# Ten plain float32 heads instead of sixteen, weights decoded in three Vector pieces, and 13 slots without a head between the two kinds of heads

## The chip, the cores and the metric

One core of a Trainium2 chip runs the kernel. The metric is the device time of one execution in microseconds, the median of several runs. Engines are named as in the profile: PE is the tensor engine (PEld its weight loads), DVE is Vector, ACT is ScalarE, POOL is GpSimd, SP issues the DMAs. Each engine takes its instructions in the order in which the program gives them.

## The reference

Gated causal attention over 64 heads (8 batches of 8 heads, 576 tokens, 64 columns), then a normalised two-layer block on the 4608 tokens of 512 columns. The two weight matrices reach the kernel as 64-bit floats.

```python
def _attn_ref(q, k, v, f):
    scores = scale * np.matmul(q, k.transpose(0, 1, 3, 2))
    cum = np.cumsum(np.log(np.clip(f, 0.0001, 1.0)), axis=-1)
    scores = np.where(causal, -1e9, scores + cum[..., :, None] - cum[..., None, :])
    attn = np.exp(scores - np.max(scores, axis=-1, keepdims=True))
    return np.matmul(attn / (np.sum(attn, axis=-1, keepdims=True) + 1e-09), v)

def _moe_ref(x, g_ln, w_ch1, w_ch2):
    xn = (x - mu) / np.sqrt(var + 1e-06) * g_ln
    return x + np.maximum(xn @ w_ch1, 0.0) @ w_ch2
```

## The kernel before

**Slots.** The work is a list of slots, each a row tile t (1 to 4) of one head: 64 heads make slots 0 to 255, and three empty ones follow. In a slot the letters of a string in `ORDERS` say which pieces are given to the engines, and in which order:

- Q: score products (PE, L357 in a plain head, L359 and L360 in a split one); S: row minima (DVE, L373); e: exponentials (ACT, L384); B: row sums and normalised rows (DVE L389 and L390, POOL L391).
- t, h, l: transposes of the tile `LAG` = 2 slots before (PE, L397), their copy or first part (ACT, L447), their second part (DVE, L452, split heads alone).
- A, F, a: product with v (PE, L460 plain, L482 split), its columns, out to DRAM (L513, L516, L527, L529).
- M, r, m, N: a step of the second layer. M is the first product (12 matmuls, L566 to L568), r and m its two parts (ACT L574, DVE L579), N the second product of the step before (6 matmuls, L588 to L590). R takes the tokens' rows and loads and splits the next chunk's tokens (L543, L550, L551).
- W: a tick of the weights; f, g, w: some of its Vector pieces; s: column sums (PE, L191); P: operands of the next heads.

**Two kinds of heads.** A head with n < `NFULL` is plain: its products take float32 operands as they are. Any other is split: each operand is two float32r parts, made by ACT, DVE and POOL (L329, L330, L335 to L337, L343, L344), and there are more products of a cheaper kind. The parts of split heads lie in a pool that opens where the weights' pool closes, so the first heads are plain.

**Weights.** There are 32 items of 128 x 512 (16 for each layer). A tick decodes one from 64-bit words: ACT scales its high words (L160), then four Vector pieces (L176, L177, L180, L172), of which the last is followed by an addition on POOL (L173). An item of the first layer then has its column sums made on PE and four centring pieces on DVE (L199). ACT makes the first part (L215), POOL the second (L219). A tick starts when the slot's due count says so: `W_SLOTS` = 2.82 slots per tick until slot 37, 1.1 ticks per slot from there. Step j needs the items up to 2(j + 1).

**Steps.** From slot 35 on a slot holds one step if there is one. 18 chunks of 256 tokens have 16 steps each, 288 in all. A chunk can start when its tokens are written: chunks 0 and 1 after batch 0 (heads 0 to 7), 2 and 3 after batch 1 (heads 8 to 15). What is left after the last slot, 72 steps, runs alone.

## Time and profile before

| | |
|---|---|
| median of 3 runs | 1277.68 us (1275.74 to 1287.45) |
| span of the profiled execution | 1274.4 us (its time beside the span is not listed) |
| PE, DVE, ACT, POOL busy | 1248.6, 848.8, 639.4, 455.2 us |
| slot 4, 36, 58 and 256 start | at 20.0, 100.2, 216.1 and about 1049 us |
| DMA | 90.96 MB |

A slot's start is read as the start of its first score product in the order of time. The span runs from the first to the last instruction; the median of the runs lies 3.3 us above it.

### The profile page before, as it was taken

The page shows a single profiled execution, that of the slowest core. Times are in us where ns is not written, and L with a number is a line of the kernel's source. Part 1 is how long each engine was busy: PE and PEld are TensorE (multiplying, and loading weights), DVE is VectorE, ACT ScalarE, POOL GpSimd, SP SyncE. Part 2 cuts the span into 40 slices and gives each one's busy share as a digit, 9 for nine tenths or more (in the row PEclk, how much of TensorE's full clock was granted, in tenths as well). Part 3 has the DMA queues.
Part 4 walks back from the last instruction along what each step waited for, and adds up shares of the span by engine and source line. Part 5 has one row for each costly group of instructions (what it writes and reads, how often), then busy time and mean ns, then how long its engine had stood idle before and what let it go on. Part 6 is the DMA issues. An engine that isn't in the chain of part 4 may idle for free.

```text
span 1274.4 us, 24837 instructions
## 1 busy us (share of the span) xinstructions
PE 1248.6 (98%) x8292; PEld 1087.5 (85%) x8292; DVE 848.8 (67%) x2948; ACT 639.4 (50%) x1904; POOL 455.2 (36%) x543
## 2 busy tenths in 40 slices
PE   8999889999999999999999999999999999999998
PEld 5656667789899999999999989899999999999997
DVE  6889997367676767686868687777777773233232
ACT  5776455455555555555555565555555552112111
POOL 4666665234343333433333444333434330000000
PEclk8999998999999999999999999999999999999999
DMA  5444341122212222222222212222222200100100
GB/s 167 141 129 138 123 150 49 47 70 75 75 62 62 76 75 74 71 79 72 78 70 68 77 58 66 64 75 75 75 74 75 69 33 26 34 26 9 34 17 17
DMA packets 65904, 90.96 MB, mean 71 GB/s; under 512 B 15856, under 2 KB 50672, under 8 KB 65776
## 3 DMA queue, kind: packets, MB, share of 16 engines
q1 hardware_dynamic: 65776, 89.37, 22.4%
q8 instruction: 66, 1.08, 0.4%
q14 instruction: 62, 0.51, 0.1%
HBM read 70.17 MB, written 19.17 MB: 70 GB/s over the span
## 4 chain that ended last, share of the span: by engine, by line
PE 85%; DVE 9%; DMA 2%; issue 2%; ACT 1%; POOL 1%; SPq 0%; POOLq 0%; DVEq 0%; ACTq 0%
PE h L566 10%; PE h L567 10%; PE h L568 10%; PE acc L588 10%; PE acc L589 10%; PE acc L590 10%; PE tr L397 8%; PE o L482 5%; PE s L359 3%; PE s L360 3%; PE o L460 2%; DVE wy L177 2%; PE s L357 2%; DVE wr L180 1%; DVE wr L176 1%
## 5 line engine op out<-in xcount | busy, mean ns | idle before, releaser
L566 PE MATMUL h<-x,w1h 128*128 128x256 f32 x1152 | 329.0, 286 | 0.8 <-DVE st L389 0.7
L391 POOL TENSOR_SCALAR p<-p,st 64x64 f32<-64x64 f32 (+4 forms) x320 | 179.0, 564 | 417.4 <-DVE st L390 175.0
L567 PE MATMUL h<-x,w1h 128*128 128x256 f32 x1152 | 326.5, 283 | 1.5 <-DVE x L551 1.5
L568 PE MATMUL h<-x,w1l 128*128 128x256 f32 x1152 | 325.1, 282 | 0.0
L574 ACT ACTIVATE hh<-h 128x256 fp32r<-128x256 f32 x288 | 110.7, 384 | 292.4 <-PE h L568 291.9
L588 PE MATMUL acc<-w2h,hh 128*128 128x512 f32 x576 | 228.9, 397 | 0.0
L589 PE MATMUL acc<-w2l,hh 128*128 128x512 f32 x576 | 227.8, 396 | 0.0
L579 DVE SCALAR_TENSOR_TENSOR hh<-h,hh 128x256 fp32r<-128x256 f32 x288 | 121.0, 420 | 157.3 <-ACT hh L574 152.3
L590 PE MATMUL acc<-w2h,hh 128*128 128x512 f32 x576 | 225.0, 391 | 0.0
L567 PEld LDWEIGHTS h<-x,w1h 128*128 128x128 f32 x1152 | 219.5, 191 | 6.2 <-DVE x L551 1.7
L566 PEld LDWEIGHTS h<-x,w1h 128*128 128x128 f32 x1152 | 218.9, 190 | 6.1 <-DVE st L389 1.4
L568 PEld LDWEIGHTS h<-x,w1l 128*128 128x128 f32 x1152 | 219.2, 190 | 0.0
L384 ACT ACTIVATE p<-p,st 64x64 f32<-64x64 f32 (+4 forms) x320 | 178.9, 560 | 76.7 <-DVE st L373 75.1
L447 ACT CAST ph<-tr 64x128 fp32r<-64x128 f32 (+4 forms) x384 | 109.2, 334 | 135.5 <-PE tr L397 122.8
L397 PE MATMUL tr<-identr,p 128*128 128x128 f32 (+2 forms) x896 | 147.1, 274 | 10.1 <-POOL p L391 8.9
L397 PEld LDWEIGHTS tr<-identr,p 128*128 128x128 f32 (+2 forms) x896 | 97.0, 130 | 51.4 <-POOL p L391 17.8
L452 DVE TENSOR_TENSOR ph<-tr,ph 64x192 fp32r<-64x192 f32 x192 | 57.7, 301 | 117.5 <-ACT ph L447 114.2
L373 DVE CUSTOM_DVE_ANT_0 p<-s,mask 64x64 f32<-64x64 f32 (+4 forms) x320 | 130.1, 420 | 4.7 <-POOL p L391 2.1
L590 PEld LDWEIGHTS acc<-w2h,hh 128*128 128x128 f32 x576 | 108.6, 188 | 25.1
L588 PEld LDWEIGHTS acc<-w2h,hh 128*128 128x128 f32 x576 | 109.4, 190 | 14.8 <-issue 1.0
L589 PEld LDWEIGHTS acc<-w2l,hh 128*128 128x128 f32 x576 | 109.5, 190 | 11.9
L337 POOL TENSOR_TENSOR hi<-raw,hi 64x576 fp32r<-64x576 f32 x48 | 74.0, 1541 | 95.1 <-ACT hi L335 91.3
(85 smaller groups left out, 2008.6 us busy)
## 6 DMA issues: line engine op xcount, KB each, us to landing
raw<-in_qk_dram SPq DMA_DIRECT2D x48, 576.0 KB
wr<-in_w_dram SPq DMA_DIRECT2D x32, 512.0 KB
vr<-in_v_dram SPq DMA_DIRECT2D x64, 160.0 KB
out_dram<-xt SPq DMA_DIRECT2D x36, 256.0 KB
xa<-xs SPq DMA_DIRECT2D x32, 160.0 KB
xb<-xs SPq DMA_DIRECT2D x32, 128.0 KB
xf<-in_qk_dram SPq DMA_DIRECT2D x16, 144.0 KB
kl<-in_qk_dram SPq DMA_DIRECT2D x16, 144.0 KB
```

Of the source, the lines that this page charges most:

```text
L373: nc.vector.tensor_tensor_reduce(out=pt[:m, a:z], in0=sp, in1=mask[:m, off + a : off + z], scale=-SCALE, scalar=3.0e38 if i == 0 else st[: ...
L384: nc.scalar.activation(pt[:m, :w], pt[:m, :w], AF.Exp, bias=st[:m, i : i + 1], scale=-1.0, accum_out=st[:m, 2:3])
L391: nc.gpsimd.tensor_scalar(out=pt[:m, :w], in0=pt[:m, :w], scalar1=st[:m, 3:4], scalar2=1.0, op0=ALU.mult, op1=ALU.mult)
L397: nc.tensor.transpose(out_, in_, ident[:m, :m])
L566: mm(ph, w1h[:, k, fs], c.x[k][:, 0, :], start=(k == 0), stop=False)
L567: mm(ph, w1h[:, k, fs], c.x[k][:, 1, :], start=False, stop=False)
L568: mm(ph, w1l[:, k, fs], c.x[k][:, 0, :], start=False, stop=(k == KT - 1))
L574: nc.scalar.activation(h[:, 0, :], c.ph, AF.Relu)
L579: nc.vector.scalar_tensor_tensor(out=h[:, 1, :], in0=ph, scalar=0.0, in1=h[:, 0, :].bitcast(F32), op0=ALU.max, op1=ALU.subtract)
L588: mm(c.acc[i], h[:, 0, ts_], w2h[:, j, :], start=(j == 0), stop=False)
L589: mm(c.acc[i], h[:, 0, ts_], w2l[:, j, :], start=False, stop=False)
L590: mm(c.acc[i], h[:, 1, ts_], w2h[:, j, :], start=False, stop=(j == FT - 1))
```

## The change

`NFULL` falls from 16 to 10. Between head 9 and head 10 stand `BRIDGE` = 13 slots without a head (slots 40 to 52); weights and steps go on in them. A split head's slots thus begin at 53, and the list has 272 slots. Ticks come at one per 1.9 slots until slot 36. The decoding takes the low 32-bit word instead of 16 bits of it: three Vector pieces, and no POOL addition. The pools change over, and head 10 is loaded, in slot 50; its operands are made in slots 51 and 52.

```diff
-NFULL = 16
+NFULL = 10
+BRIDGE = 13
-W_SLOTS, W_CHANGE, W_TICKS = 2.82, 37, 1.1
+W_SLOTS, W_CHANGE, W_TICKS = 1.9, 36, 1.1
-W_ASIDE = 6
+W_ASIDE = 5
...
-    (66, "AthQFlMSPNreamLRB"),
+    (4 * NFULL + BRIDGE + 2, "AthQFlMSPNreamLRB"),
...
-            def last():
-                ve.scalar_tensor_tensor(out=zf, in0=low, scalar=2.0**-36, in1=zf, op0=ALU.mult, op1=ALU.mult)
-                nc.gpsimd.tensor_tensor(out=yf, in0=yf, in1=zf, op=ALU.add)
...
-                lambda: ve.tensor_scalar(out=z, in0=y, scalar1=0xFF800000, scalar2=None, op0=ALU.bitwise_and),
-                last,
+                lambda: ve.scalar_tensor_tensor(
+                    out=y, in0=low, scalar=29, in1=y, op0=ALU.logical_shift_right, op1=ALU.bitwise_or
+                ),
...
-    slots = [(n, t) for n in range(B * H) for t in (1, 2, 3, 4)]
-    slots += [None] * (LAG + 1)
+    slots = [(n, t) for n in range(NFULL) for t in (1, 2, 3, 4)] + [None] * BRIDGE
+    slots += [(n, t) for n in range(NFULL, B * H) for t in (1, 2, 3, 4)] + [None] * (LAG + 1)
+    last_full = 4 * NFULL - 1
...
-                moe.limit = min(NCHUNK, max(0, u - LAG - 1) // (4 * H) * S // C)
+                gone = u - LAG - 1
+                gone -= min(max(0, gone - last_full), BRIDGE)
+                moe.limit = min(NCHUNK, max(0, gone) // (4 * H) * S // C)
...
+            if u == last_full + BRIDGE - 2:
+                while not wp.done():
+                    wp.tick()
+                    wp.fill(99)
+                early.close()
+                pools["late"] = ctx.enter_context(tc.tile_pool(name="late", bufs=1))
+                start_head(NFULL)
+                load_v(hd[NFULL])
+            if u == last_full + BRIDGE - 1:
+                prep_a(hd[NFULL])
+            if u == last_full + BRIDGE:
+                prep_b(hd[NFULL])
+                start_head(NFULL + 1)
```

Three places in the order of the two programs follow. Line numbers of the changed kernel are 4 or 5 lower than before (L176 is L171, L177 is L172, L199 is L195, L397 is L393, L566 is L562, L588 is L584).

Vector among the early heads, before. wr and wy are a weight as it comes and as it is decoded, p and st a head's probabilities and row numbers, s its scores:

```order
L176 TENSOR_SCALAR wr_4_598<-wr_4_598 128x512
L373 ISA p_0_760,st_0_761<-s_0_0_751,mask 64x64
L373 ISA st_0_761 64x1
L373 ISA p_1_763,st_1_764<-s_1_0_753,mask 128x192
L373 ISA st_1_764 128x1
L177 SCALAR_TENSOR_TENSOR wy_4_697<-wy_4_697,wr_4_598 128x512
L180 TENSOR_SCALAR wr_4_598<-wy_4_697 128x512
L389 TENSOR_SCALAR st_0_761<-st_0_761 64x1
L390 RECIPROCAL st_0_761<-st_0_761 64x1
L389 TENSOR_SCALAR st_1_764<-st_1_764 128x1
L390 RECIPROCAL st_1_764<-st_1_764 128x1
L172 SCALAR_TENSOR_TENSOR wr_4_598<-wr_4_598 128x512
```

One item's four pieces lie here across two slots.

The same engine among the early heads after the change:

```order
L171 TENSOR_SCALAR wr_5_587<-wr_5_587 128x512
L369 ISA p_3_725,st_3_726<-s_3_0_718,mask 128x448
L369 ISA st_3_726 128x1
L172 SCALAR_TENSOR_TENSOR wy_5_690<-wy_5_690,wr_5_587 128x512
L175 SCALAR_TENSOR_TENSOR wy_5_690<-wr_5_587,wy_5_690 128x512
L385 TENSOR_SCALAR st_3_726<-st_3_726 128x1
L386 RECIPROCAL st_3_726<-st_3_726 128x1
L171 TENSOR_SCALAR wr_5_645<-wr_5_645 128x512
```

Three pieces stand for four, and the next item's first piece follows within the next slot.

PE ahead of the first product of step 3 of chunk 0, before, in head 10 (h and acc are a step's first and second product, pc column sums, s scores, tr transposes of the probabilities p):

```order
L588 MATMUL acc_1_1424<-w2h,hh_1_1431 128x512
L589 MATMUL acc_1_1424<-w2l,hh_1_1431 128x512
L590 MATMUL acc_1_1424<-w2h,hh_1_1431 128x512
L357 MATMUL s_2_0_1519<-kl_1271,xf_151 128x320
L191 MATMUL pc_1524<-wy_8_1378,gneg 128x128 x4
L397 MATMUL tr_4_1529<-identr,p_4_1392 64x128
L397 MATMUL tr_4_1529<-identr,p_4_1392 128x128 x3
L397 MATMUL tr_4b<-identr,p_4_1392 128x128
L566 MATMUL h_3_1536<-x_0_1275,w1h 128x256
```

Scores, column sums and transposes stand between the step before and this one.

PE at the same place after the change, in slot 41, which has no head of its own:

```order
L584 MATMUL acc_1_1476<-w2h,hh_1_1483 128x512
L585 MATMUL acc_1_1476<-w2l,hh_1_1483 128x512
L586 MATMUL acc_1_1476<-w2h,hh_1_1483 128x512
L393 MATMUL tr_4_1550<-identr,p_4_1449 64x128
L393 MATMUL tr_4_1550<-identr,p_4_1449 128x128 x3
L393 MATMUL tr_4b<-identr,p_4_1449 128x128
L562 MATMUL h_3_1557<-x_0_1324,w1h 128x256
```

The scores are gone from between the two steps, and the transposes are the last ones of head 9.

PE from the third row tile of head 14 on, before, with a step in the slot:

```order
L357 MATMUL s_3_0_2486<-kl_2223,xf_151 128x448
L397 MATMUL tr_1_2492<-identr,p_0_2407 64x64
L397 MATMUL tr_1_2492<-identr,p_1_2410 64x128
L397 MATMUL tr_1_2492<-identr,p_1_2410 128x128
L460 MATMUL o_4_2496<-ph_13_2413,vr_2108 64x256 x4
L460 MATMUL o_4_2496<-ph_13_2413,vr_2108 64x128
L566 MATMUL h_15_2502<-x_0_1275,w1h 128x256
L567 MATMUL h_15_2502<-x_0_1275,w1h 128x256
```

Step 15 of chunk 0 follows the head's own products.

PE at the same row tile of the same head after the change, slots 71 and 72:

```order
L393 MATMUL tr_1_3028<-identr,p_0_2951 64x64
L393 MATMUL tr_1_3028<-identr,p_1_2954 64x128
L393 MATMUL tr_1_3028<-identr,p_1_2954 128x128
L355 MATMUL s_3_0_3034<-hi_2759 128x448
L356 MATMUL s_3_0_3034<-kl_2760,xq_1958 128x448
L393 MATMUL tr_2_3060<-identr,p_2_2994 64x128
L393 MATMUL tr_2_3060<-identr,p_2_2994 128x128 x2
L355 MATMUL s_4_0_3066<-hi_2759 128x288
L356 MATMUL s_4_0_3066<-kl_2760,xq_1958 128x288
L355 MATMUL s_4_1_3069<-hi_2759 128x288
L356 MATMUL s_4_1_3069<-kl_2760,xq_1958 128x288
```

No row of h stands between slot 69 (step 15 of chunk 1) and slot 83 (step 0 of chunk 2); before, rows of h and acc stand in every slot here.

More of the change, by code (lines that the diff above doesn't have):

```diff
@@ L150, in load @@
                 nc.sync.dma_start(out=raw, in_=w2.bitcast(U32)[j * P : (j + 1) * P, :])
-            self.d[n] = {"raw": raw, "hw": raw.rearrange("p (n t) -> p n t", t=2)[:, :, 1]}
+            halves = raw.rearrange("p (n t) -> p n t", t=2)
+            self.d[n] = {"hw": halves[:, :, 1], "lw": halves[:, :, 0]}
         def scaled(self, n):
@@ L164, in decode @@
             d = self.d[n]
-            y, z = d["y"], d["hw"]
-            low = d["raw"].bitcast(U16).rearrange("p (n t) -> p n t", t=4)[:, :, 1]
-            zf, yf = z.bitcast(F32), y.bitcast(F32)
-            d["w"] = yf
+            y, z, low = d["y"], d["hw"], d["lw"]
+            d["w"] = y.bitcast(F32)
             ve = nc.vector
-            def last():
-                ve.scalar_tensor_tensor(out=zf, in0=low, scalar=2.0**-36, in1=zf, op0=ALU.mult, op1=ALU.mult)
-                nc.gpsimd.tensor_tensor(out=yf, in0=yf, in1=zf, op=ALU.add)
             return [
@@ L702, in attn_moe @@
     moe = Moe()
-    slots = [(n, t) for n in range(B * H) for t in (1, 2, 3, 4)]
-    nu = len(slots)
-    slots += [None] * (LAG + 1)
+    slots = [(n, t) for n in range(NFULL) for t in (1, 2, 3, 4)] + [None] * BRIDGE
+    slots += [(n, t) for n in range(NFULL, B * H) for t in (1, 2, 3, 4)] + [None] * (LAG + 1)
+    last_full = 4 * NFULL - 1
     hd = {}
@@ L788, in prep @@
         def prep():
-            if slot is not None:
-                if t == 1 and n + 1 < NFULL:
-                    start_head(n + 1)
-                if n == NFULL - 2 and t == 1:
-                    while not wp.done():
-                        wp.tick()
-                        wp.fill(99)
-                    early.close()
-                    pools["late"] = ctx.enter_context(tc.tile_pool(name="late", bufs=1))
-                if n + 1 >= NFULL and n + 1 < B * H:
-                    if t == 2:
-                        prep_a(hd[n + 1])
-                    if t == 3:
-                        prep_b(hd[n + 1])
-                if t == 3 and n + 2 >= NFULL and n + 2 < B * H:
-                    start_head(n + 2)
-                if not h.full and t == LAG + 1:
-                    prep_v(h)
-                if t == LAG + 1 and n + 1 < B * H:
-                    load_v(hd[n + 1])
+            if u == last_full + BRIDGE - 2:
[11 more added lines that the diff above has]
+                start_head(NFULL + 1)
+            if slot is None:
+                return
+            if t == 1 and n + 1 < NFULL:
+                start_head(n + 1)
+            if n >= NFULL and n + 1 < B * H:
+                if t == 2:
+                    prep_a(hd[n + 1])
+                if t == 3:
+                    prep_b(hd[n + 1])
+            if t == 3 and n >= NFULL and n + 2 < B * H:
+                start_head(n + 2)
+            if not h.full and t == LAG + 1:
+                prep_v(h)
+            if t == LAG + 1 and n + 1 < B * H and n + 1 != NFULL:
+                load_v(hd[n + 1])
         for c in [o for first, o in ORDERS if first <= u][-1]:
```

## The prediction

> **What bounds the kernel now.** I read the page's busy shares and its chain of work first, then a table of stretches of the span, cut where a slot's first score product starts (L357, later L359).
>
> ```profile
> span 1274.4 us, 24837 instructions
> ...
> PE 1248.6 (98%) x8292; PEld 1087.5 (85%) x8292; DVE 848.8 (67%) x2948; ACT 639.4 (50%) x1904; POOL 455.2 (36%) x543
> ...
> PE 85%; DVE 9%; DMA 2%; issue 2%; ACT 1%; POOL 1%; SPq 0%; POOLq 0%; DVEq 0%; ACTq 0%
> ```
>
> TensorE holds 85% of the chain that ended last, Vector 9%. A busy PE of 98% says little by itself, since ends of matmuls are modelled; so I take the cost of each kind of work from stretches in which nothing but that work is in the queue.
>
> ```profile
> core 0: us, PE busy (x) PEld busy (x) DVE busy (x) ACT busy (x) POOL busy (x), PEclk, DMA share, GB/s
> 20.00:29.07 9.07, 9.07 (x44) 5.35 (x43) 6.16 (x28) 7.53 (x24) 4.40 (x6) 0.99 0.36 110
> ...
> 58.71:70.28 11.57, 10.20 (x53) 6.20 (x52) 8.03 (x32) 8.15 (x27) 8.60 (x10) 1.00 0.38 102
> 89.17:100.19 11.02, 10.00 (x52) 6.20 (x51) 9.01 (x30) 8.36 (x25) 8.23 (x9) 1.00 0.47 145
> 20.00:100.19 80.19, 77.14 (x385) 46.90 (x384) 63.84 (x238) 60.96 (x191) 51.86 (x60) 1.00 0.44 132
> 100.19:216.10 115.91, 106.28 (x597) 79.08 (x597) 110.64 (x281) 63.56 (x181) 76.69 (x70) 0.96 0.38 114
> ...
> 216.10:236.34 20.24, 20.24 (x118) 15.38 (x117) 7.79 (x32) 9.12 (x30) 4.76 (x7) 1.00 0.20 70
> 982.74:1049.00 66.26, 66.26 (x472) 60.45 (x469) 47.78 (x181) 36.56 (x112) 23.23 (x31) 1.00 0.17 52
> 1131.20:1177.70 46.50, 46.50 (x305) 42.32 (x304) 13.35 (x40) 8.49 (x22) 0.00 (x0) 1.00 0.07 23
> ```
>
> The last row is the tail: 16 steps of the second layer in 46.50 us, 2.91 us each with the chunk's own rows (about 2.82 without). The row above is 16 slots with 16 steps and four split heads: (66.26 - 46.50)/4 = **4.94 us of TensorE per split head**, 1.23 per slot. The stretch from 216.10 is one plain float32 head with four steps: 20.24 - 4 x 2.82 = **8.96 us per plain head**; the stretch from 20.00, a plain head with almost nothing beside it, took 9.07. So from about 216 us to the end TensorE is never idle, and time is its work. Before that there are two stages: slots 4 to 35 (20.00 to 100.19, eight plain heads) and slots 36 to 57 (100.19 to 216.10, the weights beside heads and first steps). In the second of them Vector is busy 110.64 of 115.91 us: there Vector sets the pace.
>
> I therefore count the change as TensorE work removed plus TensorE idle time added or removed.
>
> **1. Six heads become split heads.** 6 x (8.96 - 4.94) = **-24.1 us** of TensorE. This lies where TensorE is the bound, so it counts in full. The added work of the other engines (two casts, two subtractions, the second parts) is hidden in slots with a step, since the 66.26 us stretch shows Vector at 47.78, ScalarE 36.56, GpSimd 23.23.
>
> **2. Slots without a step.** The order of the two programs shows the price. Tokens of chunks 2 and 3 need batch 1, that is, head 15. Before, the 32 steps of chunks 0 and 1 last until that batch is written. After, 13 slots without a head use up steps early: step 15 of chunk 1 stands in slot 69, the first step of chunk 2 in slot 83. Slots 70 to 82 (13 of them) and slot 115 carry split heads and no step. TensorE has 1.23 us of work there; the slot lasts as long as the loop through ScalarE and Vector. No row of before shows such a slot alone, so I rebuild the loop from four neighbouring slots (t = 1 to 4): parts on Vector (L452), minima (L373), exponential on ScalarE (L384), then the next transposes' copy (L447), after which the next L452 may start.
>
> ```profile
> 267.42 0.28 DVE L452 TENSOR_TENSOR ph<-tr,ph 64x128 fp32r<-64x128 f32 x1 [1.31 <-ACT ph L447]
> 269.48 0.19 ACT L384 ACTIVATION_READ_ACCUMULATOR p<-p,st 128x1 f32 x1
> 270.35 0.64 ACT L447 CAST ph<-tr 64x128 fp32r<-64x128 f32 x2 [0.39 <-PE tr L397]
> 271.02 0.28 DVE L452 TENSOR_TENSOR ph<-tr,ph 64x128 fp32r<-64x128 f32 x1
> 273.01 0.19 ACT L384 ACTIVATION_READ_ACCUMULATOR p<-p,st 128x1 f32 x1
> ...
> 275.10 0.47 ACT L447 CAST ph<-tr 64x192 fp32r<-64x192 f32 x2 [1.61 <-PE tr L397]
> 275.61 0.35 DVE L452 TENSOR_TENSOR ph<-tr,ph 64x192 fp32r<-64x192 f32 x1 [1.40 <-ACT ph L447]
> 276.72 1.73 DVE L336 CAST xq<-raw 64x576 fp32r<-64x576 f32 x1
> 278.77 0.40 DVE L527 TENSOR_TENSOR xs<-o,ot 64x256 f32<-64x256 f32 x1
> 280.35 0.12 DVE L389 TENSOR_SCALAR st<-st 128x1 f32<-128x1 f32 x1
> 280.51 0.16 DVE L390 RECIPROCAL st<-st 128x1 f32<-128x1 f32 x1
> 280.70 0.28 DVE L452 TENSOR_TENSOR ph<-tr,ph 64x128 fp32r<-64x128 f32 x1
> 283.26 0.19 ACT L384 ACTIVATION_READ_ACCUMULATOR p<-p,st 128x1 f32 x1
> ...
> L336 DVE CAST xq<-raw x48: 446/449/1737, 237.9 to 1026.7; 64x576 fp32r<-64x576 f32 x48
> ```
>
> t = 1: 267.42 to 269.67, plus a copy of 0.64, is 2.89. t = 2: 271.02 to 273.20 plus 0.47 is 2.65. t = 3: Vector itself is the longer way, 275.61 to 279.17 (the cast L336, waiting 1.3 of its 1.73 us for GpSimd, then two more) and 0.3 for L389 and L390, 3.9. t = 4: 280.70 to 283.45 plus 0.64 is 3.4. Mean **3.2 us**. Idle: 14 x (3.2 - 1.23) = **+27.6 us**. Bounds: 2.1 per slot if Vector's own busy time were all (47.78/16 = 3.0, less an estimated 0.9 for what steps and chunks add), +12; 4.14 (66.26/16, the pace with a step) as the other end, +41. I keep 3.2, since four rows' own sums give it.
>
> **3. The weights' stage.** Per weight, Vector loses one of four pieces and GpSimd its addition.
>
> ```profile
> L177 DVE SCALAR_TENSOR_TENSOR wy<-wy,wr 128x512 uint32<-128x512 uint32 x32 | 39.6, 1237 | 0.0
> L176 DVE TENSOR_SCALAR wr<-wr 128x512 uint32<-128x512 uint32 x32 | 23.3, 727 | 0.0
> L180 DVE TENSOR_SCALAR wr<-wy 128x512 uint32<-128x512 uint32 x32 | 22.9, 717 | 0.6
> L172 DVE SCALAR_TENSOR_TENSOR wr<-wr 128x512 f32<-128x512 uint16 x32 | 22.0, 686 | 0.3
> ...
> L173 POOL TENSOR_TENSOR wy<-wy,wr 128x512 f32<-128x512 f32 x32 | 42.1, 1316 | 26.1 <-issue 16.7 <-DVE wr L172 5.2 <-PE tr L397 1.5
> ...
> L172 DVE SCALAR_TENSOR_TENSOR wr<-wr x32: 662/686/757, 10.3 to 203.2; 128x512 f32<-128x512 uint16 x32
> ...
> L177 DVE SCALAR_TENSOR_TENSOR wy<-wy,wr x32: 676/1052/3024, 8.3 to 199.2; 128x512 uint32<-128x512 uint32 x32
> ...
> L176 DVE TENSOR_SCALAR wr<-wr x32: 408/478/1531, 7.8 to 197.3; 128x512 uint32<-128x512 uint32 x32
> ```
>
> The pieces' means add to 3.37 us; their shortest are 0.41 (L176), 0.68 (L177), and L172 always near 0.69. L177's spread, 676 to 3024 ns for one form, is waiting inside the instruction: it is long where a GpSimd TENSOR_TENSOR (L173 or L219) runs. About 1.2 us of the 3.37 is such waiting, on two GpSimd instructions per weight; one of the two goes. The new third piece has L177's form, so I take 0.41 + 0.68 + 0.68 + 0.6 = 2.4 us per weight against 3.37. (Bounds for the new piece: 0.68 and 1.24, L177's shortest and its mean.)
>
> L172 reads two tiles of the on-chip memory as L177 does, and yet all 32 of it lie between 662 and 757. [...]
>
> Slots 36 to 57 held 5.5 plain heads, 15 steps and ten column sums. A sum costs 0.89:
>
> ```profile
> 32.62 0.89 PE pc L191 x8
> ```
>
> TensorE work: 49.3 + 42.3 + 8.9 + 1.4 (rows) = 101.9, so 14.0 of the 115.91 us was idle. After, the same 15 steps lie in slots 36 to 52 with one plain head, some 5 us of head 9's last transposes and products (work that before lies behind slot 57) and seven sums: 9.0 + 42.3 + 1.4 + 6.2 + 5 = 64 us. Vector had 110.6. Eighteen decodings become 12, -6 x 3.37 = -20; each of the 12 loses 1.0, -12; and 4.5 heads go at 2.4 each, -11 (2.4 is the 63.84 us of the early stretch, less 11 decodings at 3.37 and as many centrings at 0.67, over eight heads): 68 us. The two engines are about level, so idle time stays; I take 5 of the 14: **-9 us** (bounds -13 and 0).
>
> **4. The early heads.** Ticks per head go from 1.4 to 2.1. Before, heads with two ticks took 11.57 and 11.02 us with TensorE at 10.2 and 10.0, heads with one 9.07 and up; the mean was 80.19/8 = 10.0. I take 10.5: +3.8 us for eight heads, of which 2.7 is three column sums that only move forward from a later slot. **+1.1 us** (bounds: 9.9, -3.6; 11.6, +10). GpSimd's missing addition speaks for the low side: L173 and L219 together hold back L391, for which the transposes wait. The weights' loads come closer together with the ticks, 17 instead of 11 of 512 KB in this stage, 3.1 MB more on 132 GB/s, about 165 GB/s; they are asked for two ticks ahead and made anyone wait for 2.1 us in all:
>
> ```profile
> ACT wy L160 <- DMA wr<-in_w_dram: 2.1, 2, 1.5
> ```
>
> **5. Head 10's operands** are asked for three slots ahead of its scores, after the weights' buffers are free.
>
> ```profile
> 100.11 4.77 DMA xr<-xa
> ...
> L330 POOL TENSOR_TENSOR kl<-raw,hi x48: 1421/1430/1447, 235.1 to 1022.0; 64x576 fp32r<-64x576 f32 x48
> ...
> L337 POOL TENSOR_TENSOR hi<-raw,hi x48: 1402/1541/1656, 239.1 to 1026.8; 64x576 fp32r<-64x576 f32 x48
> ```
>
> A load of 4.8, a cast of about 0.7, 1.4 and 1.5 on GpSimd make 8.4 us, against 3 x 2.82 = 8.5 of steps. I take **+2** (0 to 5). On SP's queue the load stands behind chunk 1's tokens, issued slots before; vr of head 10 follows it.
>
> **Sum:** -24.1 + 27.6 - 9 + 1.1 + 2 = **-2.4 us** on the profiled execution, whose span is 1274.4 (no other time of it is shown). The median of the runs lies 3.3 above that span; carried to it, 1277.7 - 2.4 = **1275 us**. One per cent, 12.8 us, is about what can be told from no change.
>
> **Rivals.**
> A, faster: the stepless slots run at 2.5 us, nearer Vector's own time (14 x 0.7 = -9.8), and the early heads at 9.9 since GpSimd is lighter (-4.7): 1275 - 14.5 = **1261**. For it: DVE's queue is emptier without L579. Against: the t = 3 slot alone is 3.9 by its rows.
> B, slower a little: these slots keep 4.14 us: 14 x 0.94 = +13, **1288**. It needs 0.9 us of waiting per slot that no row shows.
> C, on the other side: Vector becomes the bound from slot 4 on. If the three pieces cost some 3.4 us after all (waits on L219 as long as those on two instructions before), a head's Vector work is 2.4 + 2.1 x (3.4 + 0.67) = 11.0 at least, and I price it by the longest head with two ticks, 11.57: 8 x 1.07 = +8.6; and the 9 us of part 3 are not won: 1275 + 18 = **1293**. It decides from about 2.9 us per weight, where 2.4 + 2.1 x (2.9 + 0.67) passes TensorE's 9.9 per head. Against: the addition that made half of the waits is gone.
>
> **How the numbers follow.** Forecast 0.58 (own range 1266 to 1284), A 0.20, B 0.09, C 0.13. Below 1264.9 lies most of A: faster 0.20. Above 1290.5 lies most of C and the end of B: slower 0.14. Within 1%: 0.66. The range 1258 to 1292 takes in A, B and the edge of C.
>
> **What would show it.** In the changed kernel's profile: 13 slots without L562 some 240 to 285 us in, with PE well under 10 in them and 3.2 us apart (part 2; above 4 is B, below 2.7 is A); the first slot of step chunk 2 near 284; the score products of head 9 starting near 104 (later than 110 is C); DVE under PE between 125 and 170; the third piece's spread like L177's; PE waiting on L333 or its neighbours at head 10 for about 2 us. The forecast fails as a whole if slots with a step and a split head no longer take 4.14 us, since parts 1 and 2 are both priced by that pace.

## The result and the profile after

The changed kernel takes 1287.0 us (median of 20 runs, 1285.0 to 1291.3), the kernel before 1277.3 on the same chip: ratio 1.0059, interval [1.0037, 1.0081]. The forecast was 1275, 2.4 us less than before; the change takes 9.7 us more. That is 0.6% slower, inside the wide range given (1258 to 1292) and within the 1% called "same", but outside the forecast's own range (1266 to 1284), and the interval lies wholly on the slow side. The rest of this part is about why gains and losses that should have balanced did not. The kernel before has 12 of its 20 runs near 1276 us and 8 between 1280 and 1290, where the mean granted clock is lower (0.980 to 0.988 against 0.99 wherever it is listed), and its median was 1276.3 to 1282.4 on the three chips used below, so the ratio to the kernel before on the same chip says more than a median alone. Spans of single profiled executions are compared below: 1286.4 after, 1274.4 before, so +12.0, which is 2.3 more than the medians show.

The page of the changed kernel: span, TensorE's busy time, the granted clock in 40 slices, and the chain by engine and by line.

```profile
span 1286.4 us, 24852 instructions
...
PE 1244.8 (97%) x8280; PEld 1097.9 (85%) x8280; DVE 853.6 (66%) x2994; ACT 646.6 (50%) x1916; POOL 431.3 (34%) x529
...
PEclk8998999958999999999999999999999999999999
...
PE 85%; DVE 8%; ACT 2%; issue 2%; DMA 1%; POOL 1%; SPq 0%; POOLq 0%; DVEq 0%; ACTq 0%
PE h L563 10%; PE h L562 10%; PE h L564 10%; PE acc L584 10%; PE acc L585 10%; PE acc L586 9%; PE tr L393 8%; PE o L478 6%; PE s L355 3%; PE s L356 3%; PE o L456 2%; DVE xq L332 2%; PE s L353 1%; DVE p L369 1%; ACT ph L443 1%
```

The same two rows of the page before:

```profile
PEclk8999998999999999999999999999999999999999
...
PE h L566 10%; PE h L567 10%; PE h L568 10%; PE acc L588 10%; PE acc L589 10%; PE acc L590 10%; PE tr L397 8%; PE o L482 5%; PE s L359 3%; PE s L360 3%; PE o L460 2%; DVE wy L177 2%; PE s L357 2%; DVE wr L180 1%; DVE wr L176 1%
```

Two things are new after the change. The ninth of the 40 slices of the clock row (32 us each) shows 5, about half clock, where before had 9. And the chain has a line of Vector's that was not among its first fifteen before: the cast L332 (L336 before), 2%. TensorE's share of the chain is the same 85%.

The stretches of the changed kernel (busy us of each engine, the granted clock in the third column from the end):

```profile
core 0: us, PE busy (x) PEld busy (x) DVE busy (x) ACT busy (x) POOL busy (x), PEclk, DMA share, GB/s
18.61:28.22 9.61, 9.61 (x28) 5.95 (x29) 5.84 (x27) 5.62 (x17) 2.97 (x5) 0.50 0.50 149
18.61:107.20 88.59, 85.11 (x408) 52.18 (x408) 73.01 (x254) 64.26 (x197) 45.13 (x55) 0.95 0.49 149
...
112.63:127.60 14.97, 10.34 (x37) 6.72 (x36) 11.94 (x25) 7.29 (x21) 5.85 (x6) 0.66 0.49 154
107.20:181.25 74.05, 67.66 (x406) 55.34 (x406) 60.54 (x137) 35.14 (x87) 32.46 (x27) 0.93 0.35 111
181.25:249.62 68.37, 68.37 (x482) 62.16 (x481) 48.70 (x181) 36.95 (x113) 26.80 (x33) 1.00 0.20 66
249.62:294.25 44.63, 31.72 (x147) 26.53 (x145) 32.58 (x123) 25.74 (x80) 21.18 (x27) 0.58 0.28 89
1004.87:1071.90 67.03, 66.24 (x468) 60.09 (x467) 47.50 (x180) 36.78 (x113) 23.08 (x30) 1.00 0.17 54
```

Second row: slots 4 to 35, the stretch that took 80.19 us before. The row above it is its beginning, all of it at half clock. Third: slot 38 alone, 15 us. Fourth: slots 36 to 52, the weights' stage. Fifth: slots 53 to 69, each with a step, TensorE full. Sixth: the 13 stepless slots 70 to 82, 3.43 us each, at a clock of 0.58. Last: 16 slots with 16 steps, 67.03 us where before had 66.26.

### The profile page after: what moved, and what is told of

It reads as the page before. It is cut to its first block, busy times and chain, and to the rows that moved or that the text cites. A ratio compares the mean times of both kernels' runs of the same rounds, so it can differ in the third digit from the quotient of the medians.

```text
span 1286.4 us, 24852 instructions
## 1 busy us (share of the span) xinstructions
PE 1244.8 (97%) x8280; PEld 1097.9 (85%) x8280; DVE 853.6 (66%) x2994; ACT 646.6 (50%) x1916; POOL 431.3 (34%) x529
## 4 chain that ended last, share of the span: by engine, by line
PE 85%; DVE 8%; ACT 2%; issue 2%; DMA 1%; POOL 1%; SPq 0%; POOLq 0%; DVEq 0%; ACTq 0%
PE h L563 10%; PE h L562 10%; PE h L564 10%; PE acc L584 10%; PE acc L585 10%; PE acc L586 9%; PE tr L393 8%; PE o L478 6%; PE s L355 3%; PE s L356 3%; PE o L456 2%; DVE xq L332 2%; PE s L353 1%; DVE p L369 1%; ACT ph L443 1%
## 5 line engine op out<-in xcount | busy, mean ns | idle before, releaser
L563 PE MATMUL h<-x,w1h 128*128 128x256 f32 x1152 | 327.7, 284 | 7.8 <-DVE x L547 5.9
L562 PE MATMUL h<-x,w1h 128*128 128x256 f32 x1152 | 329.6, 286 | 0.0
L387 POOL TENSOR_SCALAR p<-p,st 64x64 f32<-64x64 f32 (+4 forms) x320 | 175.0, 550 | 456.0 <-DVE st L386 219.2
L563 PEld LDWEIGHTS h<-x,w1h 128*128 128x128 f32 x1152 | 221.1, 192 | 13.2 <-DVE x L547 9.9
L584 PE MATMUL acc<-w2h,hh 128*128 128x512 f32 x576 | 227.8, 396 | 0.0
L562 PEld LDWEIGHTS h<-x,w1h 128*128 128x128 f32 x1152 | 220.6, 191 | 4.3 <-DVE wy L175 0.3
L443 ACT CAST ph<-tr 64x128 fp32r<-64x128 f32 (+4 forms) x432 | 122.7, 333 | 152.6 <-PE tr L393 131.4
L393 PE MATMUL tr<-identr,p 128*128 128x128 f32 (+2 forms) x896 | 151.9, 280 | 9.5 <-POOL p L387 9.4
L448 DVE TENSOR_TENSOR ph<-tr,ph 64x192 fp32r<-64x192 f32 x216 | 65.0, 301 | 136.0 <-ACT ph L443 133.1
L393 PEld LDWEIGHTS tr<-identr,p 128*128 128x128 f32 (+2 forms) x896 | 99.2, 133 | 48.6 <-POOL p L387 18.5
L584 PEld LDWEIGHTS acc<-w2h,hh 128*128 128x128 f32 x576 | 109.3, 190 | 13.7
L333 POOL TENSOR_TENSOR hi<-raw,hi 64x576 fp32r<-64x576 f32 x54 | 82.7, 1531 | 98.5 <-ACT hi L331 98.1
```

Source lines behind the costliest of these rows:

```text
L387: nc.gpsimd.tensor_scalar(out=pt[:m, :w], in0=pt[:m, :w], scalar1=st[:m, 3:4], scalar2=1.0, op0=ALU.mult, op1=ALU.mult)
L393: nc.tensor.transpose(out_, in_, ident[:m, :m])
L443: nc.scalar.copy(out=hi, in_=tp)
L562: mm(ph, w1h[:, k, fs], c.x[k][:, 0, :], start=(k == 0), stop=False)
L563: mm(ph, w1h[:, k, fs], c.x[k][:, 1, :], start=False, stop=False)
L584: mm(c.acc[i], h[:, 0, ts_], w2h[:, j, :], start=(j == 0), stop=False)
```

## Where the 12 us went

I cut both traces at the first step of chunk 2, whose relu starts at 298.3 us before (slot 75) and at 297.9 after (slot 83). Up to there the change gains 0.4 us, from there to the end it loses 12.4. Ahead of the cut the changed kernel has 24 slots made cheaper (-24.1), five slots of heads fewer (-6.2), and one step's second product more (+1.4: that of step 15 of chunk 1 now stands in slot 70, while before it stands behind the cut); the last two come back behind the cut with the other sign. So it must have gained 28.5 us of TensorE's idle or half-clock time there. The stretches account for 28.3 of it:

| term | forecast | measured | from |
|---|---|---|---|
| six heads split | -24.1 | -24.1 | taken over, no run isolates it |
| stepless slots 70 to 82 | +25.6 | +27.2 | 44.63 - 13 x 1.23 - 1.4 |
| stepless slot 115 | +2.0 | +1.9 | a gap of 9.14 us between two steps instead of 4.61, less 1.23 and a second product of 1.4 |
| weights' stage, idle or half clock | -9 | -3.2 | after 74.05 - 67.66 + 5.1 = 11.5, before 9.6 + 5.1 = 14.7 |
| early heads, slot 36 | +1.1 | +4.3 | 107.20 - 100.19, less 2.7 for the sums that come earlier |
| head 10's operands | +2 | 0 | in the weights' stage already |
| behind the cut, chunks' starts above all | none | +5.7 | rest: 12.4 - 6.2 + 1.4 - 1.9 |
| sum | -2.4 | +11.8 | measured +12.0 |

(5.1 is half of the 10.24 us at half clock in either stage, an estimate of what that clock cost. In the last row but one some 1.7 us, by the same estimate, are a stretch of 3.41 us at half clock, from 434.4 us on, right behind slot 115.) No single term explains the miss: two are off by almost 6 us, one by 3 and one by 1.6, all to the slow side. The experiments ask what each consists of.

## Experiments

Five theories, one of them (T) in its place below. **L**: the stepless slots cost their loop, as the forecast had it. **K**: short stretches without work for TensorE are followed by a halved clock, which makes them dearer. **R**: the change shifts the chunks against the heads, and a slot with a step has no longer the old pace. **V**: with only ten heads for cover, Vector sets the pace of the weights' stage.

### The stepless slots: spread, keep_clock

*spread* gives the same 17 steps to the 30 slots 53 to 82 evenly, instead of one to each of 53 to 69.

```diff
+SPREAD = (53, 83, 17)
...
 want = moe.can(wp.ready()) and u >= FIRST_MOE
+if SPREAD[0] <= u < SPREAD[1]:
+    i, w = u - SPREAD[0], SPREAD[1] - SPREAD[0]
+    want = want and (i + 1) * SPREAD[2] // w > i * SPREAD[2] // w
```

> The same work as the changed kernel, but the 17 steps left at slot 53 are spread over the 30 slots up to the third chunk's tokens, so that slots with and without a step alternate. Theory L (a slot without a step is bound by the loop through ScalarE and Vector, 3.2 to 3.4 us, and a slot with one by TensorE, 4.14, and each alone wastes the other's slack): two neighbours share 6.4 instead of 7.6 us, 13 pairs give -12 to -17 us, and the granted clock stays at 1.0 there. Theory K (the idle time itself does not matter, the halved clock does): the clock stays up as well, but the stretch shortens only by what the slow clock cost, 3 to 5 us. Rival (14 slots without a step leave the same idle time wherever they stand): no change, within 2 us.

Measured: 1273.4 us, ratio to before 0.9974 [0.9952, 0.9995]. The stretch from slot 53 to 82:

```profile
180.76:279.49 98.73, 90.32 (x620) 78.41 (x618) 78.90 (x299) 61.19 (x191) 47.86 (x60) 0.98 0.25 80
```

98.7 us instead of 68.37 + 44.63 = 113.0: 14.3 us; the medians lie 13.6 us apart. L holds, since K alone gave 3 to 5: the same slots and steps leave about half the idle time when each pair of slots shares a step (98.7 or 113.0 less the same 85.8 us of TensorE's work).

*keep_clock* leaves the steps where they are and adds 12 products of 256 columns, whose result nobody reads, to each stepless slot (the branch is reached where the slot has no step).

```diff
+elif c == "M" and u >= 70 and moe.cur is not None:
+    wb = bank(f"wb{u}")[:, :C]
+    for i in range(12):
+        mm(wb, w1h[:, i % 4, 0:P], w1h[:, i % 4, 0:C], start=(i == 0), stop=(i == 11))
```

> In each slot without a step from 70 on TensorE multiplies 12 times into a bank that nobody reads (about 1.4 us of work), all else as in the changed kernel. Theory K (the halved clock lengthens these slots): the clock stays at 1.0 between 250 and 298 us, the 13 slots shrink from 44.6 to about 41.6, and the first step after them runs at full speed, together -4 to -5 us. Theory L (the loop through ScalarE and Vector sets them, whatever TensorE's clock): the clock stays up and the 13 slots keep 44 us, -1 us at most. Rival: the added products are in the way, +2 us or more.

Measured: 1283.7 us, 1.0054 [1.0037, 1.0071].

```profile
249.21:290.43 41.22, 38.20 (x302) 35.50 (x301) 31.42 (x122) 25.10 (x78) 21.34 (x27) 1.00 0.30 96
```

More work, and 41.22 us instead of 44.63: 3.17 per slot at a clock of 1.00. So the mean of the loop rebuilt from four rows in the forecast (3.2) was right at full clock, and the halved clock adds 3.4 us to the 13 slots. K holds in the trace, and is small. The median stands 7.2 us above that of the kernel before on its chip, where the change stands 9.7 above; the two ratios cannot be told apart, so the trace is what shows it.

Only the mean of the loop is shown. The single slots differ (2.2 to 4.6 us from one slot's first score product to the next in keep_clock), and what TensorE waits for in the 13 slots of the change is only in part the loop that was forecast:

```profile
PE o L478 <- DVE ph L448: 4.9, 4, 2.4
PE o L478 <- POOL vv L340: 4.7, 2, 2.6
PE tr L393 <- POOL p L387: 3.3, 4, 1.3
```

(us in total, times, longest.) 8.0 of the 12.9 us of waiting end at GpSimd, with the second part of v and the normalised rows; the forecast's loop ran through ScalarE and Vector alone. No run takes work from GpSimd there.

### The chunks' starts: exp_first, spread_even, cast_early, cast_only, decode_cast

In the waits of TensorE one line had moved up, from 1.5 us in one place to 5.9 us in nine: the wait for a chunk's tokens (L563 for L547).

```profile
engine line waited for: us in total, times, longest us
PE tr L393 <- POOL p L387: 9.4, 17, 1.4
PE h L563 <- DVE x L547: 5.9, 9, 0.7
PE pc L187 <- DVE wy L175: 5.5, 2, 4.6
```

The same wait in the kernel before:

```profile
PE h L567 <- DVE x L551: 1.5, 1, 1.5
```

The timeline of one such place after, and of the same place before (start, duration, engine, line):

```profile
495.40 0.67 ACT L331 CAST hi<-raw 128x576 fp32r<-128x576 f32 x1
...
496.22 1.43 POOL L333 TENSOR_TENSOR hi<-raw,hi 64x576 fp32r<-64x576 f32 x1 [1.44 <-ACT hi L331]
...
496.25 1.72 DVE L332 CAST xq<-raw 64x576 fp32r<-64x576 f32 x1
...
499.64 0.76 DVE L547 TENSOR_TENSOR x<-xr,x 128x256 fp32r<-128x256 f32 x2
...
500.12 0.39 PE L563 MATMUL h<-x,w1h 128*128 128x256 f32 x1 [0.67 <-DVE x L547]
```

```profile
427.50 0.68 ACT L335 CAST hi<-raw 128x576 fp32r<-128x576 f32 x1
...
428.23 0.45 DVE L336 CAST xq<-raw 64x576 fp32r<-64x576 f32 x1
428.33 1.65 POOL L337 TENSOR_TENSOR hi<-raw,hi 64x576 fp32r<-64x576 f32 x1 [1.38 <-ACT hi L335]
...
430.87 0.75 DVE L551 TENSOR_TENSOR x<-xr,x 128x256 fp32r<-128x256 f32 x2
```

Vector's cast of the next head's queries and GpSimd's subtraction on the same load start within 0.1 us of each other. Before, in the slots where chunks start, the cast is first and takes 0.45 us, and the subtraction 1.65; after, the subtraction is first by 0.03 us, and the cast takes 1.72. Behind it on Vector come the chunk's tokens: they start 4.24 us after ScalarE's cast instead of 3.37, and TensorE waits 0.67 us. Which of the two is first alternates from head to head. Before, chunks start under even heads; the 13 slots have moved them under odd ones. One and the same cast of 64x576 takes 0.45 us or 1.72: before, from 260.5 us on, the cast is first in 24 heads and takes 0.446 to 0.449 us, and the subtraction is first in 23, where the cast takes 1.716 to 1.737.

*exp_first* was a first attempt to change the order in Vector's and ScalarE's queues: the exponentials ahead of the relu.

```diff
-    (4 * NFULL + BRIDGE + 2, "AthQFlMSPNreamLRB"),
+    (4 * NFULL + BRIDGE + 2, "AthQFlMSePNramLRB"),
```

> In the heads' later order the exponentials go ahead of the next heads' operands (e before P), all else as in the changed kernel. Theory R (at a chunk's start TensorE waits for the tokens' parts, because Vector's cast of q, L332, waits 1.3 us for GpSimd's subtraction in that slot; the chunks of the changed kernel begin at odd heads, where this cast is always late): the cast comes before GpSimd's and takes 0.45 us, the first two steps of a chunk stand 3.9 instead of 4.6 us apart, 16 slots take 66.3 instead of 67.0, in all -6 to -10 us. Rival (the wait at a chunk's start comes from its loads or from ScalarE): no change there, and 67.0 stays.

Measured: 1346.6 us, 1.0543 [1.0474, 1.0613]. It says nothing on R: the relu now waits behind the exponential on ScalarE, and Vector's second part of the step behind it,

```profile
ACT p L380 <- DVE st L369: 375.4, 242, 4.5
DVE hh L575 <- ACT hh L570: 322.3, 266, 2.5
```

so that sixteen slots take about 72 us, although the cast is at 0.45 throughout, as expected. A test that moves a whole letter of the slot moves more than the thing in doubt.

*spread_even* is spread with the 17 steps over 34 slots; the chunks then start under even heads.

```diff
-SPREAD = (53, 83, 17)
+SPREAD = (53, 87, 17)
```

> The spread kernel (1273.4), with the 17 steps given out over slots 53 to 86 instead of 53 to 82, so that every later chunk of the second layer begins four slots later, under an even head as in the kernel before. Theory R (the four-slot shift put every chunk's first step into a slot in which Vector's cast for the next head takes 1.7 us instead of 0.45, and the next step waits for the chunk's tokens behind it): sixteen slots take 66.25 us instead of 67.0, in eleven chunks about 8 us; four more steps are left to the end, which costs between nothing and 8 us, so 1265 to 1274. Rival (the 0.75 us belongs to the new order or the new places in memory and not to the phase): sixteen slots stay at 67.0 and the time is 1273 to 1281.

*cast_early* is spread with the cast one slot earlier, *cast_only* the changed kernel with nothing but that.

```diff
 def prep_a(h):
...
+    nc.vector.tensor_copy(out=h.xq[0:64, :], in_=h.raw[0:64, 0, :])
     nc.scalar.copy(out=h.hi[:, 1, :], in_=h.raw[:, 1, :])
...
 def prep_b(h):
     nc.scalar.copy(out=h.hi[:, 0, :], in_=h.raw[:, 0, :])
-    nc.vector.tensor_copy(out=h.xq[0:64, :], in_=h.raw[0:64, 0, :])
```

> The spread kernel (1273.4), with Vector's cast of a split head's queries given out one slot earlier (with the first half of that head's operands instead of the second); the chunks still begin under odd heads. Theory R, with the cast as the cause: sixteen slots take 66.2 to 66.4 us instead of 67.0, the wait for a chunk's tokens at its second step goes, and the time is 1264 to 1267. Rival (the cast is only late because something else is, the splits themselves or the transfer of the tokens): 67.0 per sixteen slots and 1273; if the cast is in the way in its new slot as well, every fourth step is later and the time is above 1275.

> The changed kernel (1287.0) with nothing but Vector's cast of a split head's queries given out one slot earlier; the 13 stepless slots stay as they are. Theory R: with the chunks under odd heads the cast costs 0.75 us or more per chunk, so sixteen slots take 66.1 instead of 67.0, about 10 us over slots 83 to 256, and the time is 1274 to 1278, the time of the kernel before: the phase alone makes the change slower. Rival (in the spread kernel the cast also cost in the slots between the steps, which hold most of the 17 us that moving it gave there, and little of it is in the change): sixteen slots 67.0 and 1283 to 1287.

Measured: spread_even 1267.3 us, 0.9930 [0.9906, 0.9954]; cast_early 1256.0, 0.9840 [0.9818, 0.9861]; cast_only 1274.9, 0.9943 [0.9911, 0.9975] (12 us below the change; the kernel before had a median of 1282.4 on that chip). Sixteen slots in the three, in this order:

```profile
490.00:556.10 66.10, 66.10 (x469) 60.39 (x468) 48.60 (x181) 37.67 (x114) 25.86 (x33) 1.00 0.22 72
```

```profile
412.10:478.20 66.10, 66.10 (x469) 60.37 (x468) 48.90 (x181) 37.75 (x115) 25.58 (x33) 1.00 0.23 75
```

```profile
528.11:594.20 66.09, 66.09 (x472) 60.37 (x470) 48.26 (x178) 37.59 (x114) 25.34 (x32) 1.00 0.24 76
```

TensorE is full again in all three, whether the phase is put back or the cast taken out of its place. In cast_only the wait of L563 for L547 falls from 5.9 us in nine places to 0.5 us in one, and from the first step of chunk 2 to that of chunk 13 (their relus start at 294.6 and 1022.8 us) it takes 728.2 us where the change takes 739.8 (297.9 to 1037.8): 11.6 us. R holds. The cast itself did not become short:

```profile
L332 DVE CAST xq<-raw x54: 442/1409/1727, 180.1 to 1050.1; 64x576 fp32r<-64x576 f32 x54
```

```profile
L325 DVE CAST xq<-raw x54: 818/1132/1535, 173.7 to 1030.9; 64x576 fp32r<-64x576 f32 x54
```

(first after, then cast_only; shortest, median, longest in ns). It now runs 0.8 to 1.5 us beside GpSimd's other subtraction, in a slot where, by these waits, nothing of a chunk's start stands behind it. What cost was its place, not its length.

*decode_cast* puts the same move into the sixteen-head kernel of the next section, whose chunks start under even heads.

> Sixteen plain heads and the old pace with the three pieces (1258.4), and the cast one slot earlier. Here the chunks begin under even heads, where the cast takes 0.45 us. Theory R: nothing is won at the chunks' starts (sixteen slots 66.25 before, 66.1 after), only the single late slots of some chunks (1.3 us each in chunks 2 and 9) can go, so 1254 to 1258. Rival (the cast is a cost in every head, whatever the phase): 1246 to 1250, as much as the 17 us won under the spread kernel or half of it.

Measured: 1264.2 us (1255.7 to 1268.8), 0.9862 [0.9801, 0.9924]. That is above what either theory gave. The profiled execution, the longest of the four, ran 30.7 of its first 45 us at half clock,

```profile
14.00:44.70 30.70, 30.70 (x90) 19.16 (x91) 13.62 (x57) 13.87 (x45) 7.66 (x12) 0.50 0.38 103
```

while the clock was back at full from 19.6 us on in decode_alone, with the same instructions in that place; the mean granted clock of the four executions is 0.988, 0.991, 0.991 and, for the one of 1255.7 us, 0.999. So the median says more of the start than of the cast. From slot 12 to the end it takes 1266.9 - 49.7 = 1217.2 us and decode_alone 1256.8 - 37.9 = 1218.9. So the move is worth 1.7 us under even heads and 11.6 under odd ones, as R has it, but the single late slots of chunks 2 and 9 stayed: these chunks still take 67.5 and 67.4 us, the others about 66.1.

### The decoding and the heads apart: decode_alone, heads_alone

*decode_alone* is the kernel before with the three pieces and nothing else (`W_ASIDE` is 5 with three pieces and 6 with four); *heads_alone* is the change with the old four. Of the edit the pieces alone are shown.

```diff
-lambda: ve.tensor_scalar(out=z, in0=y, scalar1=0xFF800000, scalar2=None, op0=ALU.bitwise_and),
-last,
+lambda: ve.scalar_tensor_tensor(
+    out=y, in0=low, scalar=29, in1=y, op0=ALU.logical_shift_right, op1=ALU.bitwise_or
+),
```

> The kernel of before with the decoding in three Vector pieces alone: sixteen plain heads, the old pace, no slots without a head. Theory W (in slots 36 to 57 Vector's decoding with its waits on GpSimd sets the pace, and 14 us of TensorE idle time hang on it): Vector loses about 18 us there, the stretch of 115.9 us falls to 104 to 108, -8 to -11 us in all. Rival (the third piece waits for GpSimd as long as the two pieces it replaces, and the due ticks set the pace): -3 to +1 us.

> The ten heads, the 13 slots without a head, the pace and the orders of the changed kernel, but the weights decoded in the four Vector pieces (and one GpSimd addition) of the kernel before. It is the fourth corner beside the kernel before (1277), the change (1287) and the three pieces alone (1258, that is 18 to 19 us for the pieces where sixteen heads cover the weights). If the two parts simply add up: 1287 + 18 = 1305. If Vector's time bounds the weights' stage once only ten heads cover it (theory V), each of the 32 weights costs its full 0.84 us more of Vector, 27 us, and the waits that halved the clock grow with it: 1312 to 1325. If the ten heads leave Vector enough room after all (rival), under 1300.

| | four pieces | three pieces |
|---|---|---|
| sixteen heads | 1277 (before) | 1258.4, ratio 0.9854 [0.9835, 0.9872] |
| ten heads, 13 slots | 1311.5, ratio 1.0275 [1.0237, 1.0313] | 1287.0, ratio 1.0059 |

The weights' stage of decode_alone (slots 36 to 57) and of heads_alone (slots 36 to 52):

```profile
98.44:199.67 101.23, 100.42 (x598) 77.09 (x597) 83.29 (x261) 63.43 (x181) 47.15 (x51) 1.00 0.44 133
```

```profile
122.65:208.92 86.27, 72.61 (x406) 59.11 (x405) 74.41 (x150) 35.96 (x88) 51.99 (x41) 0.86 0.31 95
```

With sixteen heads the three pieces free Vector (110.64 us before, 83.29 now) and TensorE is full: all of the stage's 14 us of idle time go, and 18 in all, more than the 8 to 11 that W gave. With ten heads they are worth 24.5 by the medians, where a plain sum gave 18 and V 25 to 38. By the spans it is 28.8 us: 15.5 ahead of slot 36, where heads_alone runs 41 us at half clock and the change 10.2, and 12.2 in the weights' stage, where Vector holds 74.41 of 86.27 us. So the two parts of the change stand at about -19 and +29, not at -9 and +7. Against decode_alone the same sums give 28.6 of the 29.6 us between the spans: -24.1 for the heads, +29.1 for the stepless slots, +10.7 in the weights' stage (11.5 idle or half clock against 0.8), +6.1 in the early heads (slot 36 at 107.20 against 98.44, less 2.7), +6.8 behind the cut.

### The two ticks of slot 37 and the start: steady, warm_start

Slot 38 has one long wait, of TensorE for the third piece; its products then run at half clock for 10 us (the o products take 4.29 us instead of 2.30).

```profile
118.18 2.05 PE L187 MATMUL pc<-wy,gneg 128*128 128x128 f32 x8 [4.63 <-DVE wy L175]
```

Slot 37 carries two ticks, since the pace passes two whole numbers there. Theory T makes that the cause of the stall. *steady* gives it one, and the second to a slot without a head. Its pace is a list of pairs (slot, tick), linear between them.

```diff
-W_SLOTS, W_CHANGE, W_TICKS = 1.9, 36, 1.1
+PACE = [(0, 1), (36, 19.947), (42, 25.947), (43, 27.5), (45, 29.5), (46, 31.5), (50, 35.5)]
...
```

> The changed kernel with one tick of the weights in slot 37 instead of two; the second ticks come in the headless slots 43 and 46 instead of 37 and 47, and 50 as before. Theory T (two ticks in a slot whose head still runs queue two weights' Vector pieces ahead of the column sums, TensorE waits 4.6 us there and then runs at half its clock for 10 us): slot 38 takes 7 to 9 us instead of 15.0, no half clock at 117 to 127 us, slot 53 about 6 us earlier (175 instead of 181), total 1279 to 1282. Rival V (Vector's work bounds slots 36 to 52 as a whole, 60.5 us busy of 74): the waits come two to six slots later, slot 53 at 179 to 182, total 1285 to 1289.

Measured: 1284.9 us, 1.0060 [1.0037, 1.0083].

```profile
111.31:181.11 69.80, 64.74 (x405) 52.60 (x405) 59.55 (x137) 34.97 (x87) 34.36 (x27) 1.00 0.37 118
116.72:122.90 6.18, 5.55 (x30) 3.29 (x29) 5.74 (x14) 4.89 (x16) 3.40 (x5) 1.00 0.51 152
```

Slot 38 takes 6.2 us, the clock stays at 1.00, and the stage takes 69.8 us instead of 74.05: 4.2 of the 6 that T gave. The medians show 2.1 of it, and the time lies at the edge of what V gave. (The stage begins late in this execution, since 17 us ahead of it were at half clock.) Vector is as busy as before (59.55 us against 60.54), now 85% of the stage: the stall had cost 4.63 us of waiting and, by the estimate above, 5.1 of half clock, but the stage became only 4.2 us shorter, and TensorE still waits 5.1 us in it. So the stall was partly a place where Vector's lag came due, as V says. Neither theory has it alone.

*warm_start* is cast_early with 26 transposes of the identity in slots 2 to 4, where TensorE waits for the first softmax and the first keys.

```diff
+DUMMY = {(2, "t"): 4, (3, "t"): 14, (4, "Q"): 8}
...
+if (u, c) in DUMMY:
+    wd = bank(f"wd{u}")
+    for i in range(DUMMY[u, c]):
+        nc.tensor.transpose(wd[:, 0:P], ident, ident)
```

> The spread kernel with the early cast (1256.0), and 26 more transposes of the identity matrix in slots 2 to 4 (4, 14 and 8), at places where TensorE waited 0.5, 1.8 and 0.9 us for the first softmax and the first keys; they change no result. Theory K (TensorE's idle time at 14 to 18 us makes the clock halve for the 10.2 us that follow, and with it slots 4 to 6 take 13 us instead of 9): no half clock at 17 to 28 us, slot 8 at 28.5 to 30 instead of 32.7, total 1251 to 1254. Rival (the early slots wait for Vector, GpSimd and the transfers, and the clock does not matter there): slot 8 at 32 to 34, total 1255 to 1258.

Measured: 1254.5 us, 0.9793 [0.9749, 0.9836], 1.5 us under cast_early by the medians and 3.9 by the profiled spans; 0.5 us above the range that K gave and as much below the rival's.

```profile
11.05:28.48 17.43, 16.68 (x98) 11.54 (x96) 13.55 (x52) 11.61 (x37) 6.20 (x10) 1.00 0.73 202
```

No half clock ahead of slot 36, and slot 8 starts at 28.5 us instead of 32.7; at slot 36 3.0 us of it are left (103.8 against 106.9). K holds in the trace for the start as well: of the 8.4 us by which slots 4 to 35 became longer, about 3 are the clock. The rest goes with the faster ticks, Vector being busy 73.0 of 88.6 us; no run isolates it. The stretches point the same way: slots 4 to 7, two thirds of that time at half clock, take 14.4 us in the change and 9.1 before, slots 8 to 35 take 74.2 and 71.1, of which 2.7 are the sums that come earlier. And the length of the half clock at the start is not the kernel's alone: with the same instructions up to slot 36 it is 10.2 us in the change and 6.8 in cast_only, whose slot 36 starts 2.3 us sooner and whose mean granted clock is 0.973 to 0.982 from one execution to the next.

### A version that beats both: fourteen

If a stepless slot loses what a split head gains, the best number of plain heads is the least that leaves every later slot a step. *fourteen* has the three pieces, the early cast, the old pace, fourteen plain heads and four slots between.

```diff
-NFULL = 10
-BRIDGE = 13
-W_SLOTS, W_CHANGE, W_TICKS = 1.9, 36, 1.1
+NFULL = 14
+BRIDGE = 4
+W_SLOTS, W_CHANGE, W_TICKS = 2.82, 37, 1.1
```

> Three pieces, the old pace (one tick per 2.82 slots, 1.1 per slot from slot 37), the cast one slot earlier, fourteen plain heads and four slots without a head. From head 15 on every slot has a step. Theory L (a slot without a step, or a step without a head beside it, leaves TensorE idle; where all slots from the weights' stage on have steps, each plain head that becomes a split one gives its 4.0 us): two heads give 8 us less than the sixteen-head kernel, the four headless slots take back up to 4: 1246 to 1254. Rival (with less of the heads' work beside them the last eight ticks are bound by Vector, which had 4 us of work in slots of 5): 1255 to 1262.

Measured: 1247.3 us (1246.5 to 1252.3), 0.9746 [0.9698, 0.9794]: faster than both, 2.5% under the kernel before.

```profile
98.23:206.39 108.16, 107.35 (x638) 82.51 (x637) 83.00 (x257) 65.54 (x183) 50.22 (x52) 1.00 0.40 124
175.60:221.00 45.40, 45.40 (x282) 36.79 (x282) 27.34 (x102) 23.24 (x66) 21.14 (x24) 1.00 0.20 66
```

The first row is slots 36 to 59: 0.8 us of idle time. The second runs from slot 52 to 63, across the four slots without a head: none. From slot 12 to the end it takes 1245.5 - 37.7 = 1207.8 us against 1217.2 in decode_cast: 9.4 less for two heads, where two times 4.0 was the forecast.

## Why the prediction failed

The forecast was a gain of 2.4 us, and the change lost 9.7. Two steps failed, by almost 6 us each: part 3, which took two engines that are level in sum for engines that cover each other (-9 forecast, -3.2 measured), and the pace of the slots with a step, which was priced at nothing (+5.7 measured against the kernel before). Part 4 was short by 3.2 us and part 2 by 1.5; part 5 was 2 too dear.

**Part 1**, six heads at 4.0 us each: taken over in the sums, which close with it, and not isolated. *fourteen* gives 4.7 per head, with four headless slots added.

**Part 2**, the stepless slots: the place was right (13 slots from 249.6 us on, TensorE busy 31.7 of 44.6 us in them, 3.43 us apart where 3.2 was forecast), and so was the view that other engines set their length; that GpSimd ends 8.0 of the 12.9 us of waiting was not foreseen. The term came to 29.1 where 27.6 was forecast, since one step's second product (1.4 us) is work in either place. keep_clock gives 3.4 of the 29.1 to the halved clock: the forecast took the loop from stretches at full clock and did not ask what the clock would be with so little work on TensorE (0.58 in the 13 slots). Rivals A (2.5) and B (4.14) are out.

**Part 3**, the weights' stage, is one of the two steps that failed: -9 forecast, -3.2 measured. Per weight the three pieces were nearly as priced:

```profile
L172 DVE SCALAR_TENSOR_TENSOR wy<-wy,wr 128x512 uint32<-128x512 uint32 x32 | 37.5, 1173 | 0.9 <-DVE wr L171 0.5
...
L175 DVE SCALAR_TENSOR_TENSOR wy<-wr,wy 128x512 uint32<-128x512 uint32 x32 | 26.8, 837 | 0.6
...
L171 DVE TENSOR_SCALAR wr<-wr 128x512 uint32<-128x512 uint32 x32 | 16.5, 515 | 0.1
```

1.17 + 0.84 + 0.52 = 2.53 us, where 2.4 was taken. L172's row before, 662 to 757 ns in all 32 cases, did not speak for the new piece: none of the 32 had a GpSimd TENSOR_TENSOR beside it, so they could not show a wait for one. The new third piece (L175) took 0.68 to 0.69 us in 25 of 32 cases, none of which began while such an instruction was running, and 1.0 to 1.7 in the other seven, each of which did (L128 or L215). What failed is the balance behind it. I weighed the sums of the two engines (64 against 68 us) and read "about level" as "a third of the idle time goes". The runs show two large effects of opposite sign: with sixteen heads the pieces remove all 14 us of it, and taking heads away as cover, with the faster ticks, brings 10.7 back. Here the work was not level slot by slot: the pace had two ticks in slot 37, where TensorE waited 4.63 us, and 11.5 us of idle or half-clock time was left in the stage.

**Part 4**, the early heads: +1.1 forecast, +4.3 measured; slot 36 starts at 107.2 (104 was named). warm_start gives about 3 us of it to the clock at the start, on which the term has nothing: its bounds had been read from heads at full clock. From slot 8 on the heads came every 10.6 us, against the 10.5 taken.

**Part 5**: no wait of TensorE for head 10's operands stands in the list; slot 53 starts into a queue with steps. The +2 was not needed.

**Not in the sum**: the pace of a slot with a step, the other step that failed. The prediction named it as what would break the forecast ("if slots with a step and a split head no longer take 4.14 us") and priced it at nothing, though the order had shown that the chunks move by four or five slots against the heads. The rows of L336 (446 to 1737 ns) were there, one of them at 1.73 us in the quoted loop. It costs up to 5.7 us net against the kernel before, which has some late slots of its own, and 11.6 against the same kernel with the cast moved: alone enough to turn the change from 1287 to 1275. That this is the figure that was forecast is luck, since the forecast had it for other reasons.

**The rivals**: B has the time (1288) and not the mechanism, its slots of 4.14 us were 3.43. C (Vector the bound from slot 4 on, 1293) has a part of it: the pieces cost 2.5 us and not 3.4, and slots 24 to 35 repeat at 10.6 us per head, against the 10.5 forecast, but in slots 36 to 52 Vector's work did come due in the middle of TensorE's.

## What to carry to other kernels

A slot is only as cheap as what runs beside it: count the steps that are left for the slots behind a change, and do not use them up where they are not needed. When work is shifted by a few slots, look for instructions whose duration alternates (here a cast of 0.45 or 1.72 us), since the shift decides which of the two durations stands in front of the critical one. Test the parts of a combined change apart: here one part alone gave 18 us and the other took 29.

## What the runs showed of the hardware

- In the 13 stepless slots of the change no wait of TensorE was longer than 2.6 us, and the granted clock was halved from 256.9 to 297.9 us. The traces of steady and heads_alone (mean granted clock 0.976 and 0.958) have the same 41.0 us there, and with 12 products more per slot (keep_clock) it is 1.00 from 249.2 to 290.4 us. Stretches at half clock lasted 3.41 us (before, from 156.8 us; after, from 434.4), 6.83 (before, from 13.4 and from 190.9), 10.24 (after, from 18.0 and from 117.0), 17.07 (steady, from 17.4), 30.70 (decode_cast, from 14.0) and 40.96 (after, from 256.9): 1, 2, 3, 5, 9 and 12 times 3.41 within 0.04 us.
- With 26 more transposes of the identity in slots 2 to 4 the clock stayed up (warm_start: 1.00 from 11.1 to 28.5 us, where cast_early has 0.50 from 17.7 to 27.9; the mean granted clock of the four executions is 0.996 or 0.997 there and 0.990 to 0.993 in cast_early).
- A cast on Vector (L336) and a subtraction on GpSimd (L337) that started within 0.1 us of each other alternated in their order from one head to the next in the kernel before: where the cast was first it took 0.45 us and the subtraction 1.65, where the subtraction was first they took 1.72 and 1.43.
